# Replacing the planner's greedy order by an explicit table in a long-convolution and linear-attention kernel

## The chip, the cores and the metric

The kernel runs on one core of a Trainium2 chip. The metric is the device time of one execution in microseconds; smaller is better. The core has five engines that run their own instruction streams and wait for each other through semaphores: PE (TensorE, matrix products; its weight loads are listed as PEld), DVE (VectorE), ACT (ScalarE), POOL (GpSimd), and SP (SyncE), which here does nothing but issue DMAs, one after the other in the order in which they are written. Every engine takes its instructions in order: one that waits holds up all that stand behind it on that engine.

## The reference, cut to what matters

Two independent halves are computed and put side by side in the output, 2048 rows of 2 x 576 columns.

```python
def _A_ref(u, log_A_real, A_imag, C_real, C_imag, log_dt, D_skip):   # u: 1 x 2048 x 576
    dt = jnp.exp(log_dt)
    A = -jnp.exp(log_A_real) + 1j * A_imag                            # 576 x 128
    C = (C_real + 1j * C_imag) * dt[:, None]
    P = jnp.exp((A * dt[:, None])[:, :, None] * pos[None, None, :])
    K = 2.0 * jnp.einsum("dn,dnl->dl", C, P).real                     # 576 filters, 2048 long
    y = irfft(rfft(u_t, 2 * L) * rfft(K, 2 * L))[:, :, :L]            # causal convolution
    return y + u * D_skip

def _B_ref(x, wqkv, w_phi, wo):                                       # 32 heads of 18
    q, k, v = split(x @ wqkv)
    pq, pk = q @ w_phi, k @ w_phi
    phi_q = concat(softmax(pq), softmax(-pq)); phi_k = concat(softmax(pk), softmax(-pk))
    kv, z = phi_k^T v, sum(phi_k)
    return ((phi_q kv) / (phi_q z + 1e-6)) @ wo
```

## The kernel before

Half A builds the 576 filters (36 groups of 16 channels: POOL builds phases by doubling, ACT takes sines and exponentials, DVE multiplies, PE sums), transforms filters and input with two-stage Fourier transforms written as small matrix products, multiplies the spectra (16 "products") and transforms back. Half B projects 16 tiles of 128 rows to keys and values, forms one 36 x 19 state per head, and then takes 16 query tiles through projection, feature map, state product, division and output projection. The large projections split each operand into two 32-bit parts of shorter mantissa ("wh" and "wl" are the two parts of the weights) and run as 14 matmuls per tile.

`body` does not emit instructions as it goes. It records 2972 operations in a `Plan`: each has an engine, or a first and a second engine where either may do it, a cost estimate, the buffers it reads and writes, and a function that emits it. `at(name, k)` names the unit of work to which an operation belongs and `step(name)` a step in it. The units that this document speaks of are:

- `fold` (L479 to L503): the key weights multiplied by the feature map's weights, with the first matmuls of the kernel; it waits for the DMAs `e<-in_wkT_dram` and `fT<-in_wphi_dram`.
- `key` and `query` (L602, L663): one tile of half B. `softmax` (L561 to L590) is used by both; its `tt` calls (L446 is where they are recorded) may run on POOL or DVE: `e<-small,e` is the second half of the feature map, `e<-e,small` the scaling of it.
- `group` (L907): one group of 16 filters, after `phases` (POOL, L876 to L892) and `waves` (ACT, L894).
- `product` (L983 to L1055): one sixteenth of a half of the spectra. In its step p2, DVE multiplies (`ac<-us,ps`, L450); in p3 two more operations for each of two `ac` buffers (`ac<-ac`, L446) may run on POOL or DVE; in p4 PE transforms the result back (`ps<-ac,ff`).
- `last` (L1061): the last transform of half A and its store.

`Plan.run` then sets the order. It keeps for each engine the operations whose inputs are there, and at each step starts the one that can start first, by cost estimates, latencies (`LAG`), a due time for each unit (the table `WANT`) shifted for each step (`LEAD`), and five further tuned numbers. Where an operation may run on two engines the planner compares the estimated ends. A buffer's slot is given by the due order, within a window.

One more thing sets the instruction stream: filler matmuls. Where the planner's own clock says that PE would wait for more than 150 ns, `emit` puts matmuls by a tile of zeros (L215, `ps<-ident,zero`, up to 256 columns wide) in front of the operation, into the buffer that this operation overwrites: as many as fit in the wait, counting 114 ns each (228 ns while its clock holds PE for not yet warm), whatever the width of the buffer. They are written into the program as it is built, so on the chip they are run whether PE would have waited there or not.

Of the kernel before, what the change touches and what calls it, by code (L numbers as in the profile page):

```python
# [13 lines left out]
ALU = mybir.AluOpType  # L14
# [144 lines left out]
class Plan:  # L159
# [9 lines left out]
    def __init__(self):  # L169
        self.ops, self.pools, self.free, self.window, self.strict = [], {}, {}, {}, {}  # L170
        self.now, self.unit, self.part = 0.0, None, None

    def tag(self, name, pool, n, window=None):
        self.pools[name], self.free[name] = pool, [0.0] * n
        self.window[name], self.strict[name] = window or n, not window

    def at(self, name, k=0):
        self.now, self.unit, self.part = WANT[name][k], (name, k), None

# [6 lines left out]
    def op(self, eng, cost, fn, r=(), w=(), with_=(), early=0.0, table=None, busy=1.0, lock=False, mode=(128, 128), add=None):  # L186
# [3 lines left out]
        for b in w:  # L190
            deps.update(b.readers)
        k = len(self.ops)
# [11 lines left out]
        self.ops.append([eng, cost, fn, deps, bufs, self.now - early - LEAD.get(self.part, 0.0), table, busy, lock and eng, (self.unit, early, self.part), mode, fill[0] if fill else None, alt, add])  # L204

    def emit(self, k, o, eng, fill=0):
        if fill:
# [6 lines left out]
            for _ in range(fill):  # L214
                self.matmul(t[0:cols, 0:n], self.zero.t[0:rows, 0:cols], self.data.t[0:rows].bitcast(BF16)[:, 0:n], start=not o[13], stop=not o[13], skip_group_check=bool(o[13]))  # L215
        o[2](eng) if o[12] else o[2]()

    def run(self):
        ops = self.ops
        n = len(ops)  # L220
        users = [[] for _ in ops]
        todo = [len(o[3]) for o in ops]
        for k, o in enumerate(ops):
            for d in o[3]:
                users[d].append(k)
        place, seen = {}, {t: 0 for t in self.free}
        low, ahead = {t: 0 for t in self.free}, {t: set() for t in self.free}
        for k in sorted(range(n), key=lambda k: ops[k][5]):
            for b in ops[k][4]:
                if id(b) not in place:  # L230
                    place[id(b)] = seen[b.tag]
                    seen[b.tag] += 1

        def slot(b, more=0):

            fr, p, tag = self.free[b.tag], place[id(b)], b.tag
            if len(fr) <= more:
                return None
            while low[tag] in ahead[tag]:
                ahead[tag].remove(low[tag])  # L240
                low[tag] += 1
            before = p - low[tag] - more
            if before >= self.window[tag]:
                return None
            if before and self.strict[tag] and before - sum(v < p for v in ahead[tag]) >= len(fr):
                return None
            return sorted(fr)[more]

# [14 lines left out]
        self.start = [0.0] * n  # L263
        ready = {e: {} for e in self.LAG}
        table, dma, done, end, mode = None, 0.0, 0, [0.0] * n, None
        self.engine = [o[0] for o in ops]

        def free(k, t):
            ready[ops[k][0]][k] = t
            if ops[k][12]:  # L270
                ready[ops[k][12][0]][k] = t

        def first(e, t, lock):
            s = max(t, at[e])
            return max(s, port["pool" if e == "dve" else "dve"]) if lock and e in port else s
        for k in range(n):
            if not todo[k]:
                free(k, 0.0)
# [828 lines left out]
```

## Time and profile before

| what | value |
|---|---|
| time, median of three runs | 590.35 us |
| the three runs | 590.35, 584.51, 590.45 us |
| the profiled execution | span 585.5 us |
| bytes moved by DMA | 119.26 MB, mean 204 GB/s |

A group's line in the profile gives the line of the kernel, the engine, the operation with its tiles, the number of instructions, their busy time together, the mean time of one, and the idle time of the engine just before them with what ended it. Matmuls overlap, so a mean of 319 ns does not say that a matmul adds 319 ns; the distance between starts does. A busy PE is no proof of useful work here, since the fillers count as busy.

### The profile page before, as it was taken

What the parts mean: (1) busy time and instruction counts of PE and PEld (TensorE: products, weight loads), DVE (VectorE), ACT (ScalarE), POOL (GpSimd) and SP (SyncE); (2) the same over time, 40 slices, a digit from 0 to 9 for tenths busy, and PEclk for the clock granted to TensorE, in tenths of its full rate; (3) what the DMA queues carried; (4) which work ended last, traced back from release to release, by engine and by line L of the source; (5) the groups of instructions that cost most, each with busy time, mean ns of one, the idle gap of its engine ahead of it and who ended that gap; (6) DMA issues with size and microseconds to landing.
All of it is one profiled execution on the core that took longest, in us unless ns stands there. A gap on an engine that the chain in (4) does not pass through costs nothing.

```text
span 585.5 us, 18811 instructions
## 1 busy us (share of the span) xinstructions
PE 558.6 (95%) x7694; PEld 461.4 (79%) x7694; DVE 516.7 (88%) x1110; ACT 392.5 (67%) x672; POOL 239.3 (41%) x385
## 2 busy tenths in 40 slices
PE   5999999999999999898999999999999999999996
PEld 4898899999987679787786776767678786767885
DVE  4799999999999899999899999999978788787751
ACT  5479868687778989488678586998685334432332
POOL 0437366844763446671551448544601210201000
PEclk9899999999999999899999999999999999999999
DMA  8979822550239485226655846885589789997586
GB/s 270 270 254 305 314 89 80 176 160 8 68 94 286 162 289 186 77 88 167 213 207 168 250 148 200 234 247 179 178 242 302 211 234 302 277 303 262 182 260 207
DMA packets 91317, 119.26 MB, mean 204 GB/s; under 512 B 9826, under 2 KB 73186, under 8 KB 91230
## 3 DMA queue, kind: packets, MB, share of 16 engines
q1 hardware_dynamic: 91230, 118.04, 64.9%
q8 instruction: 61, 1.00, 0.7%
q14 instruction: 26, 0.21, 0.1%
HBM read 68.76 MB, written 49.26 MB: 202 GB/s over the span
## 4 chain that ended last, share of the span: by engine, by line
PE 59%; DVE 19%; DMA 9%; ACT 8%; issue 2%; POOL 1%; SPq 1%; ACTq 0%; DVEq 0%
PE ps L431 55%; DVE cs L924 2%; DVE E L925 2%; DMA zi<-dram 2%; PE ps L215 2%; PE ps L678 2%; DVE e L446 1%; DVE ac L450 1%; ACT cs L904 1%; DMA kb<-dram 1%; DMA e<-in_wkT_dram 1%; DVE E L927 1%; ACT cs L903 1%; DVE E L929 1%; DMA dt<-in_ldt_dram 1%
## 5 line engine op out<-in xcount | busy, mean ns | idle before, releaser
L431 PE MATMUL ps<-wh,x 128*128 128x288 f32 (+2 forms) x1008 | 240.7, 319 | 2.3 <-ACT zi L436 1.8
L431 PEld LDWEIGHTS ps<-wh,x 128*128 128x128 f32 x1008 | 173.2, 188 | 12.2 <-issue 3.7
L431 PE MATMUL ps<-wl,x 128*128 128x288 f32 (+2 forms) x560 | 174.9, 313 | 0.0
L888 POOL TENSOR_TENSOR cs<-cs,pi 128x128 int32<-128x128 int32 (+4 forms) x180 | 117.7, 657 | 10.7
L431 PEld LDWEIGHTS ps<-wl,x 128*128 128x128 f32 x560 | 105.7, 189 | 0.7
L579 POOL TENSOR_TENSOR o<-e 128x576 f32<-128x576 f32 x32 | 42.0, 1320 | 98.5 <-ACT e L576 92.2
L918 ACT ACTIVATE ps<-ps 128x512 f32<-128x512 f32 x108 | 57.0, 585 | 11.3 <-PE ps L431 11.1
L924 DVE TENSOR_TENSOR cs<-ps,cs 128x1024 f32<-128x1024 f32 x36 | 43.6, 1212 | 5.5 <-ACT ps L918 5.4
L431 PEld LDWEIGHTS ps<-kvb,fT 126*128 126x128 f32 (+1 forms) x320 | 40.2, 196 | 7.2 <-PE ps L431 1.7
L450 DVE TENSOR_TENSOR ac<-us,ps 128x576 f32<-128x576 f32 x64 | 44.5, 744 | 0.5 <-ACT fT L436 0.5
L898 ACT ACTIVATE cs<-cs 128x1040 f32<-128x1040 int32 x35 | 37.6, 1073 | 10.7 <-POOL cs L888 10.5
L431 PE MATMUL ps<-kvb,fT 126*128 126x133 f32 (+1 forms) x320 | 42.8, 285 | 0.9 <-DVE small L571 0.6
L925 DVE TENSOR_TENSOR E<-ps,cs 128x1024 f32<-128x1024 f32 x36 | 43.5, 1208 | 0.1
L446 POOL TENSOR_TENSOR ac<-ac 128x288 f32<-128x288 f32 x21 | 17.2, 826 | 63.8 <-DVE ac L450 63.8
L431 PEld LDWEIGHTS ps<-E,cs 128*32 128x32 f32 x2304 | 34.5, 110 | 10.4 <-issue 3.9
L431 PE MATMUL ps<-E,cs 128*32 128x64 f32 x2304 | 40.7, 221 | 1.1 <-ACT zi L436 0.7
L576 ACT ACTIVATE e<-e 128x1152 f32<-128x1152 f32 x32 | 37.0, 1173 | 6.6 <-DVE e L446 4.8
L904 ACT ACTIVATE cs<-cs,hp 128x1040 f32<-128x1040 f32 x36 | 41.4, 1149 | 0.0
L215 PE MATMUL ps<-ident,zero 128*128 128x256 bf16 (+6 forms) x230 | 33.1, 292 | 6.5 <-DVE cs L924 4.3
L903 ACT ACTIVATE cs<-cs 128x1040 f32<-128x1040 int32 x36 | 38.3, 1064 | 0.2
L436 ACT ACTIVATE zi<-ps 128x288 f32<-128x288 f32 x73 | 25.1, 417 | 16.1 <-PE ps L431 15.6
L568 DVE TENSOR_REDUCE small<-ps 128x16 f32<-128x288 f32 (+2 forms) x64 | 28.5, 445 | 8.0 <-PE ps L431 7.1
(140 smaller groups left out, 1046.9 us busy)
## 6 DMA issues: line engine op xcount, KB each, us to landing
xd<-x SPq DMA_DIRECT2D x16, 576.0 KB
dram<-zi SPq DMA_DIRECT2D x16, 576.0 KB
x<-xd SPq DMA_DIRECT2D x16, 576.0 KB
dram<-zi SPq DMA_DIRECT2D x32, 288.0 KB
kb<-dram SPq DMA_DIRECT2D x32, 288.0 KB
ub<-dram SPq DMA_DIRECT2D x32, 288.0 KB
dram<-zo SPq DMA_DIRECT2D x32, 288.0 KB
zi<-dram SPq DMA_DIRECT2D x16, 576.0 KB
```

Of the source, the lines that this page charges most:

```text
L215: self.matmul(t[0:cols, 0:n], self.zero.t[0:rows, 0:cols], self.data.t[0:rows].bitcast(BF16)[:, 0:n], start=not o[13], stop=not o[13], ski ...
L431: pe.matmul(o, l, r, start=start, stop=stop, skip_group_check=skip)
L450: op(eng, c_dve(n) if eng == "dve" else c_pool(n), lambda: e.tensor_tensor(dst(), a(), b(), op=alu), r=r, w=w, lock=eng == "pool" or not a ...
L576: op("act", c_act(1152) + 40, lambda: act.activation(e.t, e.t, AF.Exp), r=[e], w=[e], table="exp")
L579: op("pool", c_pool(470), lambda: pool.tensor_tensor(pair.t, e.t[:, :, :, 0:9], e.t[:, :, :, 9:18], op=ALU.add), r=[e], w=[pair], lock=True)
L888: op("pool", c_pool(2 * n * W), lambda n=n, j=j: pool.tensor_tensor(x()[:, :, :, n:2 * n], x()[:, :, :, 0:n], pi.t[:, j:j + 2, gs].bitcast ...
L898: op(("act", "dve"), (c_act(65 * W), c_dve(65 * W)), lambda e, cs=cs, x=x: act.activation(cs.t[:, 0], x(), AF.Abs) if e == "act" else dve. ...
L903: act.activation(cs.t[:, 1], cs.t[:, 1].bitcast(I32), AF.Sin, scale=TURN)
L904: act.activation(cs.t[:, 0], cs.t[:, 0], AF.Sin, scale=-TURN, bias=hp.t)
L918: op("act", c_act(512), lambda: act.activation(ps.t, ps.t, AF.Exp), r=[ps], w=[ps], table="exp")
L924: op("dve", c_dve(64 * W), lambda: dve.tensor_tensor(F(), both(M.t), F(), op=ALU.mult), r=[M, cs], w=[cs])
L925: op("dve", c_dve(64 * W), lambda: dve.tensor_tensor(E.t[:, :, :, 32:64], both(up.t), cs.t[:, :, :, 0:32], op=ALU.mult), r=[up, cs], w=[E])
```

## The change

The operations, their functions and their buffers stay as they are. What `run` decided step by step is now read from a table, `ORDER`: 2972 numbers, each the place of an operation in the order of recording; a star behind a number says that it runs on its second engine. The due times, the step shifts, the windows and the five tuned numbers go. The cost estimates, latencies and the clock that counts them stay, and serve two ends only: they choose the free buffer slot, and they set the number of fillers ahead of a PE operation, by the same rule as before. The clock now also makes each PE operation wait for the two tiles that fillers read, and the first key tile for the clearing of its sum.

```diff
-    def run(self):
+    def run(self, order):
         ops = self.ops
...
-        while done < n:
-            best = None
-            for e, rs in ready.items():
...
-            e, k, s = best
+        for x in order:
+            k, second = int(x.rstrip("*")), x.endswith("*")
             o = ops[k]
+            e, cost = o[5] if second else o[:2]
+            s = max([at[e], *(end[d] for d in o[3])])
             for b in o[4]:
                 if b.t is None:
                     fr = self.free[b.tag]
                     b.t0 = min(fr)
                     fr.remove(b.t0)
-                    ahead[b.tag].add(place[id(b)])
+                    s = max(s, b.t0)
                     b.t = self.pools[b.tag].tile(b.shape, b.dt, name=b.tag, tag=b.tag)
...
-            nf = 0
+            fill = 0
             if e == "pe":
                 t = at[e]
                 if o[11] is not None:
-                    t = max(t, 0.0 if o[13] else o[11].t0, self.zero_at)
+                    t = max(t, 0.0 if o[12] else o[11].t0, self.zero_at)
                     idle(t - at[e])
                     c = FILL if self.warm else 2 * FILL
-                    nf = max(0, min(100, int((s - 150.0 - t) // c)))
+                    fill = max(0, min(100, int((s - 150.0 - t) // c)))
...
-STAY, TURNOVER, NEAR, LEAN_POOL, LEAN_ACT = 37.6104, 135.5510, 109.2559, -92.0902, 57.9818
-LEAD = dict(g1=1412.5796, g2=445.7536, ...
-WANT = dict(
...
+ORDER = """
+384 2 3 0 362 1 363 1313 1312 1316 1317 40 1314 1315 46 1322 5 364* 4 7 12 1225 1321 365* 1281 19 1324 1319 33 41
...
+""".split()
...
     with tc.manual_schedule():
-        pl.run()
+        pl.run(ORDER)
```

What the built programs hold, counted over the whole of each: fillers 230 before, 91 now (up to the first two large projections 79 before and 37 now; in the rest of the kernel 151 and 54). DVE has 1110 operations of its own before and 1064 now, POOL 381 and 429, ACT 584 and 582. Moved from DVE to POOL, net: 19 of `ac<-ac`, 14 of `e<-small,e`, 7 of `e<-e,small` 128x1152, 6 of `e<-e,small` 128x576, 2 of `x<-zo,x`. ACT's table loads are 34 before and 38 now. SP issues the same 395 DMAs.

Three places follow. Names are the program's: `v` and `sel` hold a selection matrix that half A needs first at its first group, `ub<-in_u` an input block of half A, `zo<-in_xT` a tile of half B's input, `zi`, `cs<-in_wv` the value weights, `dt`, `th`, `cre`, `cim` filter parameters. All lines below L460 or so stand two lines earlier in the changed file.

The first place is the head of SP's queue, up to the first two blocks of key weights. Before:

```order
L802 DMA v_85<-in_sel_dram 128x512
L746 DMA ub<-in_u_dram 128x576
L473 DMA zo<-in_xT_dram 128x5x128
L821 DMA dt<-in_ldt_dram 128x96
L823 DMA th<-in_aim_dram 128x96
L823 DMA cre<-in_cre_dram 128x96
L823 DMA cim<-in_cim_dram 128x96
L802 DMA v_115<-in_sel_dram 128x512
L473 DMA zi<-in_wv_dram 128x5x192
L473 DMA cs<-in_wv_dram 128x5x192
L482 DMA fT<-in_wphi_dram 128x630
L486 DMA e<-in_wkT_dram 126x640 x2
```

And the same stretch of SP's queue now:

```order
L471 DMA zo<-in_xT_dram 128x5x128
L821 DMA th<-in_aim_dram 128x96
L819 DMA dt<-in_ldt_dram 128x96
L471 DMA zi<-in_wv_dram 128x5x192
L821 DMA cre<-in_cre_dram 128x96
L821 DMA cim<-in_cim_dram 128x96
L471 DMA cs<-in_wv_dram 128x5x192
L484 DMA e<-in_wkT_dram 126x640
L480 DMA fT<-in_wphi_dram 128x630
L484 DMA e<-in_wkT_dram 126x640
L744 DMA ub<-in_u_dram 128x576
```

Both loads of `sel` and the load of `u` now stand behind the first key weights, which move from the twelfth place to the eighth.

The second place is PE's first work, between the first `fold` blocks and the first large projection. Before, the piece behind the last of nine fillers, up to the first of the next six:

```order
L215 LDWEIGHTS zero
L215 MATMUL ps<-ident,zero 128x256
L431 MATMUL ps<-fT,E 128x126 x5
L431 MATMUL ps<-fT,kvb 128x72 x5
L215 LDWEIGHTS zero
L215 MATMUL ps<-ident,zero 128x256
```

Now, from the first `fold` blocks on:

```order
L429 MATMUL ps<-fT,e 128x126 x10
L215 LDWEIGHTS zero
L215 MATMUL ps<-ident,zero 128x126
L429 MATMUL ps<-fT,E 128x126
L215 LDWEIGHTS zero
L215 MATMUL ps<-ident,zero 128x256
L429 MATMUL ps<-fT,kvb 128x72 x4
L429 MATMUL ps<-fT,E 128x126 x4
L429 MATMUL ps<-ub,w_173 128x288 x4
L429 MATMUL ps<-fT,kvb 128x72
```

One filler stands where nine stood, another one in the middle of the blocks, and an input transform of half A (`ub,w`) has moved between them.

The third place is step p3 in the first products. On DVE before, in the first of them (`ac<-us,ps` is p2, `ac<-ac` is p3; `x` and `fT`, `ot` belong to query tiles that run beside it):

```order
L450 TENSOR_TENSOR ac<-us_4892,ps 128x576 x2
L450 TENSOR_TENSOR x_4941<-ps,x_4941 128x512
L446 TENSOR_TENSOR ac<-ac 128x288
L450 TENSOR_TENSOR x_4941<-ps,x_4941 64x128
L446 TENSOR_TENSOR ac<-ac 128x288
L436 COPY fT<-ps 126x512
L450 TENSOR_TENSOR ac<-us_4893,ps 128x576 x2
L436 COPY fT<-ps 72x256
L446 TENSOR_TENSOR ac<-ac 128x288
L436 COPY ot<-ps 128x288
L446 TENSOR_TENSOR ac<-ac 128x288
```

On POOL now, in the first two products (`cs<-cs,pi` is the doubling of phases of later groups, `o<-e` a sum in a feature map):

```order
L886 TENSOR_TENSOR cs<-cs,pi 128x16x2x16
L444 TENSOR_TENSOR ac<-ac 128x288 x3
L444 TENSOR_TENSOR e<-small,e 128x576
L577 TENSOR_TENSOR o<-e 128x576
L444 TENSOR_TENSOR ac<-ac 128x288 x3
L882 COPY cs<-pi 128x16x2
L444 TENSOR_TENSOR ac<-ac 128x288
L881 MEMSET cs 128x16
L886 TENSOR_TENSOR cs<-cs,pi 128x16x2
```

Four p3 operations stood on DVE among the copies of a query tile; now seven of the eight of two products stand on POOL, nearly in a row. In the first eight products 18 of 32 p3 operations ran on DVE before and 5 do now; in the last eight 25 and 19.

More of the change, by code (lines that the diff above doesn't have):

```diff
@@ L214, in emit @@
             for _ in range(fill):
-                self.matmul(t[0:cols, 0:n], self.zero.t[0:rows, 0:cols], self.data.t[0:rows].bitcast(BF16)[:, 0:n], start=not o[13], stop=not o[13], skip_group_check=bool(o[13]))
-        o[2](eng) if o[12] else o[2]()
-    def run(self):
+                self.matmul(t[0:cols, 0:n], self.zero.t[0:rows, 0:cols], self.data.t[0:rows].bitcast(BF16)[:, 0:n], start=not o[12], stop=not o[12], skip_group_check=bool(o[12]))
+        o[2](eng) if o[5] else o[2]()
+    def run(self, order):
         ops = self.ops
[L220 to L247, printed above, removed]
+        if sorted(int(x.rstrip("*")) for x in order) != list(range(len(ops))):
+            raise RuntimeError("the order does not hold every operation once")
         at = {e: 0.0 for e in self.LAG}
@@ L262, in busy @@
                 self.warm = True
[L263 to L275, printed above, removed]
```

222 lines of the change are left out of this document (129 added, 93 removed).

## The prediction

> **What bounds the kernel now.** I read the page first for who is busy, then the chain of waits, then stretches of the span engine by engine, the fillers by themselves, and the rows of the operations that change engines.
>
> From the page of the kernel before: the span, each engine's busy time, PE and DVE in 40 slices, the clock that PE was granted, the start of the chain that ended last, and the fillers' group.
>
> ```profile
> span 585.5 us, 18811 instructions
> PE 558.6 (95%) x7694; PEld 461.4 (79%) x7694; DVE 516.7 (88%) x1110; ACT 392.5 (67%) x672; POOL 239.3 (41%) x385
> ...
> PE   5999999999999999898999999999999999999996
> ...
> DVE  4799999999999899999899999999978788787751
> ...
> PE 59%; DVE 19%; DMA 9%; ACT 8%; issue 2%; POOL 1%; SPq 1%; ACTq 0%; DVEq 0%
> ...
> L215 PE MATMUL ps<-ident,zero 128*128 128x256 bf16 (+6 forms) x230 | 33.1, 292 | 6.5 <-DVE cs L924 4.3
> ```
>
> PE is the bound, though not through all of its 558.6 us: 33.1 us of them are fillers, which compute nothing. With the 26.9 us in which PE is idle (585.5 - 558.6), PE does no useful work in 60.0 us. The change leaves every real matmul, so those 60 us are what an order can win or add to. The stretches say where they lie: all instructions first, then the fillers (L215) alone, five stretches each.
>
> ```profile
> core 0: us, PE busy (x) PEld busy (x) DVE busy (x) ACT busy (x) POOL busy (x), PEclk, DMA share, GB/s
> 0.00:14.00 14.00, 7.34 (x43) 5.63 (x44) 6.43 (x18) 7.07 (x10) 0.78 (x10) 0.97 0.86 265
> 14.00:50.00 36.00, 36.00 (x224) 33.72 (x224) 30.92 (x81) 24.18 (x41) 15.48 (x25) 0.92 0.85 274
> 50.00:150.00 100.00, 99.90 (x1619) 91.62 (x1618) 96.99 (x202) 77.75 (x117) 61.34 (x97) 1.00 0.45 147
> 150.00:440.00 290.00, 275.49 (x4247) 221.04 (x4246) 276.16 (x569) 228.61 (x385) 143.04 (x237) 0.99 0.61 186
> 440.00:585.50 145.50, 139.88 (x1567) 109.35 (x1566) 106.25 (x243) 54.84 (x123) 18.62 (x17) 0.99 0.83 254
> ```
>
> ```profile
> core 0: us, PE busy (x) PEld busy (x), PEclk, DMA share, GB/s
> 0.00:14.00 14.00, 7.00 (x42) 5.27 (x42) 0.97 0.86 265
> 14.00:50.00 36.00, 5.62 (x37) 3.96 (x37) 0.92 0.85 274
> 50.00:150.00 100.00, 0.00 (x0) 0.00 (x0) 1.00 0.45 147
> 150.00:440.00 290.00, 20.50 (x151) 14.11 (x151) 0.99 0.61 186
> 440.00:585.50 145.50, 0.00 (x0) 0.00 (x0) 0.99 0.83 254
> ```
>
> Three regimes. Up to 50 us PE waits for the first data: in the first 14 us all but one of its 43 matmuls are fillers, and 5.62 us go in fillers after that. From 50 to 150 us PE is full (99.90 of 100). From 150 to 440 us PE loses 14.5 us idle and 20.5 us in fillers, 35.0 in all, and the engine with least slack is DVE: 276.16 of 290 us busy. From there to the end PE loses 5.6 us and there is no filler.
>
> **The change, part by part.**
>
> *The start.* The chain that ended last, in order of time, begins with DMAs (start, length, what):
>
> ```profile
> 0.74 2.77 DMA v<-in_sel_dram
> ...
> 6.23 7.30 DMA e<-in_wkT_dram
> 13.67 4.61 PE ps L431 x20
> 18.27 1.84 PE ps L215 x9
> 20.11 2.19 PE ps L431 x20
> ...
> 25.39 2.29 PE ps L215 x20
> ```
>
> The first key weights are the twelfth issue, at 6.23 us; the first issue is at 0.74, so one takes (6.23 - 0.74) / 11 = 0.50 us. As eighth issue they go out 4 x 0.50 = 2.0 us sooner. By bytes it is more (KB of each issue, from the list of DMA issues):
>
> ```profile
> ub<-in_u_dram SPq DMA_DIRECT2D x16, 288.0 KB
> ...
> v<-in_sel_dram SPq DMA_DIRECT2D x3, 256.0 KB
> ```
>
> Two loads of `sel` (`v`) and one of `u`, 256 + 256 + 288 KB, no longer run ahead, and at the 265 GB/s of that stretch they take 3.1 us. Between 2.0 and 3.1 I take 2.5 us for the first real matmul. The 42 fillers ahead of it are hidden by that wait, so the ten that go there are worth nothing.
>
> *Fillers from 14 to 50 us.* 37 become 5. A filler costs 5.62 / 37 = 0.152 us here, so at most 32 x 0.152 = 4.9 us go; nothing, if PE now waits bare for the same blocks of weights. Since the blocks come 2.5 us sooner, half of the wait should go: 2.4 us.
>
> *Fillers from 150 to 440 us.* 151 become 54, so 97 go. By the stretch's row one costs 20.50 / 151 = 0.136 us; by the longest run in the chain above 2.29 / 20 = 0.115 us. That is 11.1 to 13.2 us, and I take 12. None of it is won if the wait behind the fillers stays, and this is the term to defend. The fillers' own row names DVE as what ended most of the idle time that was left before them (4.3 of 6.5 us), and DVE has 13.8 us of slack in these 290. These are the rows of what leaves DVE, then of the same operations on POOL (instructions, busy time, mean ns of one, idle time before):
>
> ```profile
> L446 DVE TENSOR_TENSOR e<-e,small 128x1152 f32<-128x1152 f32 x16 | 23.6, 1477 | 0.0
> ...
> L446 DVE TENSOR_TENSOR e<-small,e 128x576 f32<-128x576 f32 x26 | 20.2, 776 | 0.2
> L446 DVE TENSOR_TENSOR ac<-ac 128x288 f32<-128x288 f32 x43 | 20.2, 490 | 0.1
> ...
> L446 DVE TENSOR_TENSOR e<-e,small 128x576 f32<-128x576 f32 x12 | 9.9, 827 | 0.2
> ```
>
> ```profile
> L888 POOL TENSOR_TENSOR cs<-cs,pi 128x512 int32<-128x512 int32 x36 | 41.7, 1159 | 2.4
> ...
> L446 POOL TENSOR_TENSOR ac<-ac 128x288 f32<-128x288 f32 x21 | 17.2, 826 | 63.8 <-DVE ac L450 63.8
> ...
> L446 POOL TENSOR_TENSOR e<-small,e 128x576 f32<-128x576 f32 x6 | 7.2, 1207 | 3.3 <-DVE small L571 3.3
> ...
> L446 POOL TENSOR_TENSOR e<-e,small 128x576 f32<-128x576 f32 x4 | 5.1, 1270 | 17.5 <-DVE small L450 13.5 <-DVE zo L436 3.9
> ```
>
> DVE gets rid of 19 x 0.490 + 14 x 0.776 + 7 x 1.477 + 6 x 0.827 = 35.5 us over the kernel, some 7% of its 516.7. The 13 `ac<-ac` of the first eight products, which lie in this stretch, are 6.4 us of it. So DVE's need there can fall by the 12 us by which the stretch is to shrink; the cover that a full DVE gave to PE's waits goes with it. What is late next is POOL: it takes on 19 x 0.826 + 14 x 1.207 + 6 x 1.270 = 40.2 us and seven operations of a form that it never ran, between 7 x 1.27 (the half as wide one) and twice that: 9 to 18 us. Its 239.3 us become about 293. It was idle for half of this stretch (143.04 of 290), so I cost it at nothing; the price without that cover is the second rival.
>
> *PE's bare idle time*, 14.5 us in this stretch and 5.6 at the end, I leave as it is: the table removes foreseen waits, and these were not foreseen, or fillers would stand there. Bounds: all 14.5 may go, or as much come in.
>
> *ACT.* Four more table loads. Their two largest groups:
>
> ```profile
> L903 ACT ACT_TABLE_LOAD x14 | 18.0, 1283 | 0.2
> L918 ACT ACT_TABLE_LOAD x13 | 16.7, 1283 | 1.2 <-PE ps L431 0.9
> ```
>
> 4 x 1.283 = 5.1 us on an engine that has 290 - 228.61 = 61 us free in the middle: nothing, and 5.1 us lost if each stands before a sine for which DVE waits.
>
> *SP and the last stretch.* The issues are the same 395, in another order. SP takes them in order, so a store that waits for its copy holds the loads behind it; in the last stretch the DMA engines are busy for 0.83 of the time, and there I expect neither gain nor loss, -3 to +6 us by PE's own 5.6 us of slack.
>
> The sum: 2.5 + 2.4 + 12 = 16.9 us less than 585.5, a span of 568.6 us. The runs shown are 584.51 to 590.45 with a median of 590.35; the profiled execution lies 1.0 above the lowest and 4.9 below the median. The median to come may sit on either side of such a step, so I add 1.4 us and forecast **570.0 us**.
>
> **The rivals.**
>
> *Bare waits in place of fillers.* The table is built with the same estimates as the planner; where those are wrong, PE still waits, only idle. For it: a full DVE in the middle, and PE's idle 26.9 us, which the estimates missed already. Against it: DVE does lose work. Only the start is then won: 585.5 - 2.5 = 583 us, with the 1.4 us 584.4, no measurable change. If half of the 2.4 + 12 us returns, 577.
>
> *PE cools down.* Fillers keep PE busy; without them a long bare wait may cost more than itself. The longest wait of PE, and the longest run of fillers in the middle (from the list of PE's waits: total, times, longest; and from the chain):
>
> ```profile
> PE ps L431 <- DMA e<-in_wkT_dram: 5.1, 1, 5.1
> ```
>
> ```profile
> 360.32 2.92 PE ps L215 x26
> ```
>
> After that wait of 5.1 us the next 20 matmuls took 4.61 us, 20 of their kind shortly after (half of them narrower) 2.19: 2.4 us lost on top. If six waits came back bare and long, 6 x 2.4 = 14.4 us would eat the gain: 584 us. Against it: the longest run in the middle covers 2.92 us, less than the 5.1 that did cost. The Trainium skill, "TensorE: Matmul & The Clock Gate", section "What's actually happening", says that PE falls to half its clock after an idle window of about 3.4 us and comes back after as long a busy one; the trace agrees at its one long wait (twice the time behind it), and by this rule, too, a bare wait of 2.92 us is just short of costing anything.
>
> *POOL becomes the bound; slower.* In the third place of the change seven p3 operations stand on POOL among phases and sums of feature maps. With all four on POOL, a product's p4 comes 4 x 0.826 - 2 x 0.826 = 1.7 us later than with two on each engine; with a chain of phases ahead (five links, each as wide again as the one before; the last alone takes 1.159 us, so some 2.3 us in all, an estimate) 4.0 us. Over the first eight products that is 32 us: 585.5 - 16.9 + 32 = 601 us, if nothing hides it. It decides once PE waits more than 16.9 / 8 = 2.1 us a product for POOL. Against it: PE has query tiles and groups to do in between, and POOL was idle for half of the stretch. The rows of before show another price: of the two `ac<-ac` on POOL in one product, the one that ran beside the same operation on DVE took longer (start, length):
>
> ```profile
> 328.47 0.81 POOL L446 TENSOR_TENSOR ac<-ac 128x288 f32<-128x288 f32 x1 [1.30 <-DVE ac L450]
> ...
> 330.38 1.02 POOL L446 TENSOR_TENSOR ac<-ac 128x288 f32<-128x288 f32 x1
> ```
>
> 0.21 us for each of the 48 operations that POOL gains would be 10 us of POOL's time, hidden like the rest. The Trainium skill, "SBUF — State Buffer", section "Who interferes with whom", says that a DVE instruction with two inputs in SBUF and a POOL instruction that reads SBUF lock each other out for a whole instruction; the trace shows 0.21 us here, less than the 0.490 of DVE's `ac<-ac`. By the rule the moves also take such instructions off DVE, so it speaks for neither side.
>
> *More than the fillers.* If DVE's need alone sets the middle, it shrinks by more, up to all 35.0 us that PE loses there; with half of the bare waits gone as well (7 us) and all 4.9 us of the early fillers it is 585.5 - 2.5 - 4.9 - 13.2 - 7 = 558 us, with the whole 35.0 us 543.
>
> **How the numbers follow.** The forecast, 562 to 578 us: 0.55. More won, under 562: 0.14. Half or less, 578 to 584: 0.12. Bare waits, no change: 0.10; PE cooling, no change: 0.02. POOL, slower: 0.07. About 1% is what a measurement of this kernel can tell from no change, so faster is below 584.4: 0.55 + 0.14 + 0.12 = 0.81; the same up to 596.3: 0.10 + 0.02 = 0.12; slower 0.07. Two in ten may be left out: half of the cases below 562 and the upper part of the last two, which gives 554 to 586 us.
>
> **What would show it.** Right: the fillers' group at 91 and some 12 us; the first real matmul near 11 us; DVE near 485 us and POOL near 295 us busy; PE idle no more than about 27 us in the whole span; the last group of filters done some 17 us sooner. Wrong: idle time of PE released by DVE or POOL where fillers stood (bare waits); p4's matmuls waiting for POOL's `ac` (the second rival); a granted clock under 0.9 outside the first 50 us.

## The result, and the profile after

The changed kernel takes 583.37 us (median of 20 runs, 577.81 to 590.03); before took 589.67 us beside it (20 runs). The ratio is 0.9898, 95% interval 0.9873 to 0.9924: about 1% shorter, 6.3 us where 16.9 were forecast. All ratios here leave out the slower executions of both kernels, so they differ a little from those of the medians. The profiled execution has a span of 578.1 us against 585.5. That of after belongs to an execution of 580.1 us, 3.3 under the median.

The page of the kernel after, span, busy time, and PE and DVE in 40 slices:

```profile
span 578.1 us, 18504 instructions
...
PE 539.4 (93%) x7555; PEld 445.8 (77%) x7555; DVE 499.5 (86%) x1064; ACT 392.4 (68%) x674; POOL 288.6 (50%) x433
...
PE   3999899999889998989999999999999989889996
...
DVE  4899899999889899999999999999978779778662
```

DVE's busy time falls by 17 us and POOL's rises by 49. PE's slices now show gaps (8 instead of 9) in the 5th, 11th, 12th and 16th slice, where before had none, and in the 33rd, 35th and 36th. The same five stretches as before, all instructions:

```profile
core 0: us, PE busy (x) PEld busy (x) DVE busy (x) ACT busy (x) POOL busy (x), PEclk, DMA share, GB/s
0.00:14.00 14.00, 5.29 (x40) 5.12 (x41) 6.78 (x23) 6.50 (x10) 0.71 (x9) 1.00 0.81 228
14.00:50.00 36.00, 35.25 (x273) 33.24 (x274) 33.54 (x77) 28.27 (x45) 21.05 (x35) 1.00 0.88 288
50.00:150.00 100.00, 93.76 (x1582) 85.55 (x1579) 95.32 (x195) 80.31 (x120) 65.89 (x95) 1.00 0.45 147
150.00:440.00 290.00, 277.28 (x4245) 222.46 (x4244) 266.22 (x550) 233.74 (x399) 171.70 (x267) 1.00 0.64 196
440.00:578.10 138.10, 127.83 (x1425) 99.44 (x1423) 97.64 (x225) 43.61 (x102) 29.29 (x28) 0.99 0.80 247
```

And the fillers (L215) alone in them:

```profile
0.00:14.00 14.00, 3.52 (x32) 3.35 (x32) 1.00 0.81 228
14.00:50.00 36.00, 1.02 (x5) 0.58 (x5) 1.00 0.88 288
...
150.00:440.00 290.00, 8.05 (x54) 5.17 (x54) 1.00 0.64 196
```

Read against the same rows of before, PE's time without real work (idle and fillers) goes from 13.7 to 12.2 us in the first stretch (14.00 - 5.29 + 3.52), from 5.6 to 1.8 in the second and from 35.0 to 20.8 in the fourth. But it rises from 0.1 to 6.2 us between 50 and 150 us, and from 5.6 to 10.3 in the last stretch. The stretches end at fixed times, not at the same work, so here beside them is when PE starts its last step of the n-th unit of a kind to be done (us, worked out from the starts of PE's instructions in the two traces; a group pair is two groups of 16 filters):

| PE's last step of | before | after | after - before | change since the row above |
|---|---|---|---|---|
| the 1st key tile | 55.0 | 48.9 | -6.1 | -6.1 |
| the 16th key tile | 206.3 | 203.5 | -2.8 | +3.3 |
| the 18th group pair | 454.7 | 443.3 | -11.4 | -8.6 |
| the 16th `last` | 579.2 | 571.6 | -7.6 | +3.8 |

So 14.7 us are won at the start and in the middle, and 7.1 are given back: 3.3 while the keys are done, 3.8 in the last stretch. Up to 1.7 of the 8.6 us are no matter of order: in this execution of before PE ran at half clock from 241.8 to 245.2 us, and after's did not. PE's waits of after from 50 to 150 us (line, released by: total, times, longest):

```profile
PE ps L429 <- issue: 2.1, 2, 1.9
PE ps L429 <- DVE E L923: 1.6, 2, 1.2
PE ps L429 <- DVE zi L434: 0.8, 1, 0.8
PE ps L429 <- DVE e L448: 0.7, 1, 0.7
PE ps L429 <- DVE E L927: 0.6, 2, 0.5
```

These rows are 5.8 of the 6.2 us. Wherever an engine is named, it is DVE, for 3.7 us ("issue" names none). From 440 us on it is three single waits, at 513, 468 and 499 us:

```profile
PE ps L429 <- DVE zo L434: 1.6, 1, 1.6
PE ps L429 <- DMA kb<-dram: 1.5, 1, 1.5
PE ps L429 <- ACT x L437: 1.2, 1, 1.2
```

One more difference is on DVE itself. Small operations of the filter parameters (128x96, all in SBUF), in before:

```profile
L834 DVE TENSOR_SCALAR pi<-th 128x96 f32<-128x96 f32 x18 | 3.5, 227 | 0.0
...
L834 DVE TENSOR_SCALAR dt<-mx 128x96 f32<-128x96 f32 x6 | 1.7, 286 | 0.0
...
L450 DVE TENSOR_TENSOR mn<-mn,dt 128x96 f32<-128x96 f32 x6 | 1.6, 272 | 0.1
```

and in after:

```profile
L832 DVE TENSOR_SCALAR pi<-th 128x96 f32<-128x96 f32 x18 | 7.4, 413 | 0.0
...
L448 DVE TENSOR_TENSOR mn<-mn,dt 128x96 f32<-128x96 f32 x6 | 3.6, 608 | 0.0
...
L832 DVE TENSOR_SCALAR dt<-mx 128x96 f32<-128x96 f32 x6 | 3.4, 567 | 0.0
```

The same instructions take about twice as long on average beside a busier POOL. The mean mixes two kinds: of the 18 `pi<-th` of after, the 11 that no POOL instruction overlaps in time take 193 ns on average, and the 7 that one overlaps 760 ns (198 to 2291).

### The profile page after: what moved, and what is told of

Read it like the earlier page. It is cut to its first block, busy times and chain, and to the rows that moved or that the text cites. A ratio compares the mean times of both kernels' runs of the same rounds, so it can differ in the third digit from the quotient of the medians.

```text
span 578.1 us, 18504 instructions
## 1 busy us (share of the span) xinstructions
PE 539.4 (93%) x7555; PEld 445.8 (77%) x7555; DVE 499.5 (86%) x1064; ACT 392.4 (68%) x674; POOL 288.6 (50%) x433
## 5 line engine op out<-in xcount | busy, mean ns | idle before, releaser
L886 POOL TENSOR_TENSOR cs<-cs,pi 128x128 int32<-128x128 int32 (+4 forms) x180 | 116.4, 650 | 10.1
L916 ACT ACTIVATE ps<-ps 128x512 f32<-128x512 f32 x108 | 60.0, 588 | 12.9 <-PE ps L429 12.6
L444 POOL TENSOR_TENSOR ac<-ac 128x288 f32<-128x288 f32 x40 | 32.8, 831 | 55.9 <-DVE ac L448 45.5
L429 PEld LDWEIGHTS ps<-kvb,fT 126*128 126x128 f32 (+1 forms) x320 | 38.8, 189 | 5.3 <-issue 3.1
L429 PE MATMUL ps<-kvb,fT 126*128 126x133 f32 (+1 forms) x320 | 41.4, 278 | 0.2
L429 PE MATMUL ps<-sel,mg 128*128 128x512 f32 x108 | 38.0, 430 | 3.6 <-DVE wl L496 1.6
L444 POOL TENSOR_TENSOR e<-small,e 128x576 f32<-128x576 f32 x20 | 23.3, 1167 | 33.7 <-DVE e L448 27.3
L429 PE MATMUL ps<-kb,fk 128*64 128x288 f32 x256 | 35.7, 414 | 4.2 <-DVE zo L434 1.6
L444 POOL TENSOR_TENSOR e<-e,small 128x576 f32<-128x576 f32 (+1 forms) x17 | 27.0, 1590 | 23.5 <-DVE small L448 17.1
L901 ACT ACTIVATE cs<-cs 128x1040 f32<-128x1040 int32 x36 | 38.3, 1064 | 0.2
```

Source lines behind the costliest of these rows:

```text
L429: pe.matmul(o, l, r, start=start, stop=stop, skip_group_check=skip)
L444: op(eng, [c_dve(n[0]) if e == "dve" else c_pool(n[1]) for e in eng], lambda e: (dve if e == "dve" else pool).tensor_tensor(dst(), a(), b( ...
L886: op("pool", c_pool(2 * n * W), lambda n=n, j=j: pool.tensor_tensor(x()[:, :, :, n:2 * n], x()[:, :, :, 0:n], pi.t[:, j:j + 2, gs].bitcast ...
L901: act.activation(cs.t[:, 1], cs.t[:, 1].bitcast(I32), AF.Sin, scale=TURN)
L916: op("act", c_act(512), lambda: act.activation(ps.t, ps.t, AF.Exp), r=[ps], w=[ps], table="exp")
```

## The experiments

Each time stands beside runs of the kernel before on the same chip. The ratio to compare with is that of after, 0.9898. Where an experiment on before's order has an edit of the changed kernel's text, that order is written as a table for the changed kernel, which gives the instruction streams of before; line numbers then differ by some lines.

**No fillers planned.** In each kernel the number of fillers is set to zero.

```diff
-                    nf = max(0, min(100, int((s - 150.0 - t) // c)))
+                    nf = 0
```

> The kernel before without its 230 fillers; all else in the same order. Theory A (a filler is a price: what is taken out of PE's stream is won, the premise of the prediction): 33 us of fillers go, of which the 7 ahead of the first matmul are hidden, so 590 becomes about 564. Theory B (fillers only stand in waits that last as long without them): within 1% of before, PE's idle time rises by about the 33 us that the fillers took, or the kernel is some us slower where PE cools.

Measured: 661.89 us, ratio 1.1225 (1.1172 to 1.1279). This is no measure of the fillers. Where a planner decides as it goes, the clock that counts fillers also tells it whether PE is warm, so without them it put the work in another order and on other engines (DVE has 1116 operations instead of 1110). The granted clock is 0.94 in the profiled execution. The run leaves its question open.

The same line in after, where the table holds the order whatever the clock says:

```diff
-                    fill = max(0, min(100, int((s - 150.0 - t) // c)))
+                    fill = 0
```

> The changed kernel without its 91 fillers. Theory A: 12.6 us of fillers go, 3.5 of them hidden at the start: 583 becomes about 574. Theory B: 583 within 3 us, PE's idle time rises from 38.7 to about 50 us.

Measured: 580.49 us, ratio 0.9844 (0.9798 to 0.9891). Slots of buffers may differ too, so the next pair is cleaner.

**Engines and order apart.** The order of after with the engine that before gave to each operation that may run on DVE or POOL (62 go back to DVE, 14 to POOL), and the reverse. Only stars in the table change; operation 53 is one of them:

```diff
-... 52* 1230* 53 206 55 37 ...
+... 52* 1230* 53* 206 55 37 ...
```

> The changed kernel's table with every operation that may run on DVE or POOL on the engine that it had before (62 go back to DVE, 14 to POOL); the order stays. Theory C (what POOL takes on slows DVE's operations with two inputs in SBUF, so the moves are worth little): 583 within 3 us or faster, and DVE's small parameter operations are back at a mean near 270 ns from 350. Theory D (the moves are what wins; DVE sets the middle): slower, 590 to 600.

> The kernel before in its own order, with every operation that may run on DVE or POOL on the engine that the changed kernel gives it. Theory C: no faster than before, 586 to 595. Theory D: faster, 573 to 583, since DVE sheds the same work.

Measured: 599.03 us, ratio 1.0148 (1.0096 to 1.0201), and 596.97 us, ratio 1.0133 (1.0086 to 1.0179). The two pages, after's order first:

```profile
span 593.5 us, 18729 instructions
...
PE 555.8 (94%) x7676; PEld 458.0 (77%) x7676; DVE 527.8 (89%) x1112; ACT 394.4 (66%) x674; POOL 241.7 (41%) x385
```

```profile
span 594.5 us, 18989 instructions
...
PE 569.0 (96%) x7790; PEld 468.4 (79%) x7790; DVE 494.6 (83%) x1062; ACT 392.7 (66%) x672; POOL 288.0 (48%) x433
```

Neither part wins anything alone; by the ratios both lose more than 1%. The new order needs the shorter DVE: with DVE back at 527.8 us it is 2.5% slower than after. And a shorter DVE (494.6 us) gives the old order nothing: from PE's last step of the 1st key tile to that of the 16th it needs 161.2 us, before 151.3. What it waits for there was not found; PE's waits name POOL only once, for 0.3 us. Two things go with the order in these runs and are not taken apart: 182 further operations that after gives to the other of ACT and DVE, and the fillers, which the clock counts anew (212 in the first run, 326 in the second).

**Fillers counted but not sent.** The clock counts the fillers as before, so order, engines and slots are unchanged, and only the matmuls by zeros are missing. Before and after:

```diff
-            self.emit(o, e, nf)
+            self.emit(o, e, 0)
```

```diff
-            self.emit(o, e, fill)
+            self.emit(o, e, 0)
```

> The kernel before with its fillers counted by the planner's clock as ever, so that order, engines and buffer slots stay the same, and not emitted: only 230 matmuls of zeros are missing. Theory A (a filler is a price): about 564. Theory B (fillers stand in waits that last as long without them, and PE does not cool): 585 to 592, PE's idle time up by about 30 us. Theory B2 (they hold PE's clock): slower, over 595, with a granted clock under 0.97.

> The changed kernel with its 91 fillers counted and not emitted, order and slots the same. Theory A: about 574. Theory B: 580 to 585. Theory B2: over 588.

Measured: 588.45 us, ratio 0.9977 (0.9948 to 1.0006), and 580.0 us, ratio 0.985 (0.9801 to 0.990). All 230 fillers of before, 33.1 us of PE's busy time, are worth 0.2% (by the interval no more than 0.5%), and the 91 of after some 0.5%, less than their intervals tell apart. Much of the wait that they fill is there without them: PE's idle time in before rises from 26.9 to 45.1 us. The profile of before without fillers shows a second thing, from 190 to 250 us (columns as above; the granted clock is the third number from the right):

```profile
190.00:250.00 60.00, 52.59 (x642) 43.46 (x643) 51.68 (x111) 46.86 (x80) 32.14 (x50) 0.86 0.53 170
```

Before, with its fillers, and after have in the same 60 us:

```profile
190.00:250.00 60.00, 55.01 (x840) 46.80 (x837) 55.95 (x116) 48.44 (x83) 32.64 (x53) 0.97 0.54 176
```

```profile
190.00:250.00 60.00, 55.26 (x957) 46.99 (x956) 56.26 (x121) 51.51 (x95) 43.26 (x64) 1.00 0.55 175
```

Without fillers PE loses (1 - 0.86) x 60 = 8.4 us of clock here, with them 1.8, in after none. So in this execution a filler is not idle ballast, since part of what it costs in busy time it saves in clock. How much it saves on average is not shown: the granted clock over the whole of this execution, 0.983, is near the lowest of its twelve (0.982 to 0.993). What is shown is the sum, which is close to zero.

**The small operations of the parameters.** 126 operations of DVE on the filter parameters become a maximum over one element of one input, to see whether POOL holds that up, too. What they computed is left out by it, so the filters are others.

```diff
-            tt("dve", z or (lambda: dst.t), lambda: x.t, lambda: y.t, alu, [x, y], [dst], BW)
+            op("dve", c_dve(BW), lambda: dve.tensor_reduce((z() if z else dst.t), x.t[:, :, None], axis=AX.X, op=ALU.max), r=[x, y], w=[dst], lock=True)
...
-            op("dve", c_dve(BW, True), lambda: dve.tensor_scalar(z() if z else dst.t, x.t, s0, s1, op0=o0, **k), r=[x], w=[dst], lock=True)
+            op("dve", c_dve(BW, True), lambda: dve.tensor_reduce(z() if z else dst.t, x.t[:, :, None], axis=AX.X, op=ALU.max), r=[x], w=[dst], lock=True)
```

> The kernel before with DVE's 126 small operations on the filter parameters (96 columns, one or two inputs in SBUF) replaced by a maximum over one element of their first input, which has one input in SBUF and takes about as long by itself; the filters are wrong by it. Order and POOL stay. Theory P (DVE and POOL lock each other out, and the change has more of it): the small operations fall from a mean near 270 to near 200 ns, and the time by 2 to 6 us, to 584 to 588. Theory T (the order is tight, the lockout only fills waits): no change, within 2 us of before.

> The changed kernel with the same replacement. Theory P: it wins more here than in the kernel before, 7 to 13 us, to 570 to 576, and PE's idle time from 50 to 150 us falls from 6.2 to under 3. Theory T: 580 to 584, the distance to the kernel before with the same replacement stays 4 to 8 us.

Measured: 587.51 us, ratio 0.9955 (0.9925 to 0.9986), and 580.33 us, ratio 0.9846 (0.981 to 0.9883). In the order of after the replaced instructions now take (413 and 567 ns before):

```profile
L832 DVE TENSOR_REDUCE pi<-th 128x96 f32<-128x96 f32 x18 | 4.2, 240 | 0.0
...
L832 DVE TENSOR_REDUCE dt<-mx 128x96 f32<-128x96 f32 x6 | 1.5, 242 | 0.0
```

That takes 10.7 us from DVE (499.5 to 488.8) and 4.3 in before's order (516.7 to 512.4), but both kernels gain about the same half per cent. So being held up by POOL is real, as these rows show, and it is not what separates the two orders.

**Less for DVE in the key tiles.** If DVE is what the new order waits for in the first 200 us, it should gain from a shorter DVE there, and before should not. First the smallest value is left out:

```diff
-            op("dve", c_dve(DH * m), lambda: dve.tensor_reduce(ends.t[:, :, 1], v(), axis=AX.X, op=ALU.min), r=[p], w=[ends])
+            op("dve", c_dve(DH * m), lambda: dve.tensor_reduce(ends.t[:, :, 1], v(), axis=AX.X, op=ALU.min) if total else
+               dve.memset(ends.t[:, :, 1], 0.0), r=[p], w=[ends])
```

> The order and the engines of before. In the key tiles each smallest value over the features (the second of the two reductions on DVE, 540 ns for 21 heads and 350 ns for 11, so 0.89 us a tile and 14.3 us in 16 tiles) is replaced by a memset to zero in the same place: the second exponential then subtracts nothing, and the division by its sum makes up for it. Theory D (in after DVE is what the stretch from 14 to 150 us waits for, and PE is not; in before PE is full there): before gains little from it, 0 to 3 us, since PE had 0.1 us of 100 free in 50 to 150 us; ratio to before 0.995 to 1.000. Theory S (a shorter DVE helps whatever the order, because DVE's queue also sets the middle): 5 to 10 us gained, ratio 0.983 to 0.991.

> The same replacement in the order and with the engines of after. Theory D: the 6.2 us in which PE has no work between 50 and 150 us fall to 2 or less, a unit's last step there comes 4 to 8 us sooner, and the end comes 4 to 8 us sooner than after's own: ratio to before 0.976 to 0.984 (after alone 0.990), so the gap to the same edit in before grows to 1.3% or more. Theory S: the same gain as in before, 5 to 10 us, so that the gap between the two orders stays at about 1.0%. If PE's idle time in 50 to 150 us stays at 4 us or more, DVE's length isn't what it waits for, and theory D falls.

Measured: 588.43 us, ratio 0.9973 (0.9934 to 1.0012), and 579.6 us, ratio 0.9809 (0.977 to 0.9849). The stretch from 50 to 150 us, before's order and after's:

```profile
50.00:150.00 100.00, 100.00 (x1620) 91.88 (x1619) 92.22 (x203) 77.93 (x118) 61.90 (x97) 1.00 0.44 142
```

```profile
50.00:150.00 100.00, 95.81 (x1591) 88.69 (x1590) 88.06 (x200) 81.50 (x122) 67.01 (x97) 0.98 0.46 149
```

The times come out as theory D has them; the idle time of PE does not. It falls from 6.2 to 4.2 us and not to 2 or less, and with 4 us or more the theory was to fall: by this mark it does. Even that fall is no pure gain, since PE runs at half clock from 54.3 to 57.7 us here (0.98 in the row) and so is busy for up to 1.7 us longer with the same work. So twice the dose, the sum of the features and its reciprocal as well; the key features are then not divided by their sums:

```diff
-        op("dve", c_dve(576), lambda: dve.tensor_reduce(sm.t.rearrange("p h s -> p s h"), pair.t, axis=AX.X, op=ALU.add), r=[pair], w=[sm])
+        op("dve", c_dve(576), lambda: dve.tensor_reduce(sm.t.rearrange("p h s -> p s h"), pair.t, axis=AX.X, op=ALU.add) if total else
+           dve.memset(sm.t, 1.0), r=[pair], w=[sm])
...
-            op("dve", 470, lambda: dve.reciprocal(sm.t, sm.t), r=[sm], w=[sm])
+            op("dve", 470, lambda: dve.memset(sm.t, 0.1), r=[sm], w=[sm])
```

> The order and engines of before. In the key tiles alone three DVE instructions become small memsets: the smallest value (0.89 us a tile), the sum over the features (0.74 us) and the reciprocal of that sum (0.54 us), about 1.85 us a tile net and 30 us in 16 tiles, all in the first 205 us. The key features are therefore not divided by their sums; everything else is computed. Theory D (DVE's load is what after's order waits for in the first 150 us, and before's order, with PE full there, cannot use a shorter DVE): 0 to 4 us gained; ratio 0.993 to 1.000. Theory S (the load is worth the same in either order): 8 to 14 us gained, ratio 0.976 to 0.986.

> The same three memsets in the order and with the engines of after. Theory D: PE's time without work in 50 to 150 us falls below 3 us (6.2 in after, 4.2 with the smallest value alone left out), the 16th key tile's last step comes 5 us or more sooner than in after, and the end 8 to 12 us sooner than after's own: ratio 0.970 to 0.977, and the gap to the same edit in before grows to 1.8% or more. Theory S: the gap stays at 1.0%. Third way, W: what DVE holds up was already given free by the smallest value alone, so it ends as that kernel did, ratio 0.978 to 0.984, with 4 us idle left in 50 to 150 us; then what is left there is not DVE's load but the order itself.

Measured: 591.19 us, ratio 1.0004 (0.997 to 1.0037), and 580.98 us, ratio 0.9829 (0.9776 to 0.9883). Before's order and after's:

```profile
50.00:150.00 100.00, 100.00 (x1620) 91.89 (x1619) 83.67 (x202) 77.68 (x117) 62.26 (x100) 1.00 0.45 145
```

```profile
50.00:150.00 100.00, 95.50 (x1591) 88.59 (x1590) 85.66 (x199) 81.23 (x122) 66.57 (x98) 0.98 0.46 150
```

In before, DVE's load falls by 13 us in this stretch (96.99 to 83.67) and the time does not move: PE, busy all the time, is the bound. In after the second dose adds nothing to the first that can be told (theory W), and some 4 us of idle PE are left; half clock, from 146.0 to 149.4 us, has its part in this row as well. The tiles themselves are the cleaner measure. From PE's last step of the 1st key tile to that of the 16th it is 154.6 us in after, 152.4 with one dose and 151.9 with two; in before's order 151.3, 151.2 and 151.7. The run that changes after only behind 440 us (the next one) has 154.7, so this measure repeats. Of the 3.3 us that after's order loses here, DVE's load thus accounts for 2.2 to 2.7, and the rest is open.

**Three waits of the last stretch.** The PE steps that wait in the rows above (the two p2 of product 12, the p1 of product 10, the two p2 of product 15) come later on PE, behind work that does not hang on them. Of the table, at the first of them:

```diff
-... 764 2770 977 978 779 2772 2777 2739 979 780 2913 2771 ...
+... 764 977 978 779 979 780 2913 2770 2772 2739 2777 2771 ...
```

> After with three PE steps of the last stretch one place later, behind work that does not hang on them: the two multiplications of product 12 with kb (the first waits 1.5 us for a DMA at 468 us), the first step of product 10 (waits 1.2 us for a buffer that ScalarE empties, at 499 us), and the two multiplications of product 15 (wait 1.6 us for a buffer that VectorE empties, at 513 us). The engines stay. Theory L (the 4.3 us of these three waits are single late releases next to ready work): PE's idle time from 440 us on falls from 10.3 to about 6 us, and the end comes 3 to 4 us sooner; ratio to before 0.983 to 0.986. Theory Q (every other step stands as tightly, so the waits only move to the steps that now come later): no gain, -1 to +3 us against after; ratio 0.988 to 0.995.

Measured: 583.1 us, ratio 0.9867 (0.9825 to 0.9908): no gain that can be told from after. The last stretch and its longest waits:

```profile
440.00:582.20 142.20, 133.77 (x1464) 103.39 (x1463) 100.49 (x230) 45.30 (x106) 29.32 (x28) 0.99 0.80 246
```

```profile
PE ps L440 <- ACT fT L445: 1.1, 1, 1.1
PE ps L440 <- DMA zi<-dram: 0.7, 1, 0.7
...
PE ps L440 <- DMA kb<-dram: 0.3, 1, 0.3
```

The wait for `kb` shrinks to 0.3 us, and others come up, for steps that wait for ACT and for `zi`. With the 18 fillers that the clock adds (2.7 us), PE is without work for 11.1 us here, 10.3 before this edit. The ratio, 0.9867, lies between what theory L (0.983 to 0.986) and theory Q (0.988 to 0.995) have, and its interval takes in both; what speaks for Q is that PE's time without work did not fall.

**What helps, put together.** The smallest value left out and the fillers not sent, in the order of after.

```diff
-            self.emit(o, e, fill)
+            self.emit(o, e, 0)
...
-            op("dve", c_dve(DH * m), lambda: dve.tensor_reduce(ends.t[:, :, 1], v(), axis=AX.X, op=ALU.min), r=[p], w=[ends])
+            op("dve", c_dve(DH * m), lambda: dve.tensor_reduce(ends.t[:, :, 1], v(), axis=AX.X, op=ALU.min) if total else
+               dve.memset(ends.t[:, :, 1], 0.0), r=[p], w=[ends])
```

> The order of after with the smallest value left out of the key tiles' softmax (as in the run before last batch's) and the 91 fillers not sent to PE. The output is the same, since a sum divides the shift out. If the two edits add up, 0.9809 less the 0.5% that the unsent fillers gave: ratio 0.974 to 0.978, some 576 us. If a filler costs nothing and its 0.5% was spread between runs: 0.979 to 0.983.

Measured: 577.47 us, ratio 0.9771 (0.9723 to 0.982), the shortest of all: 2.3% under before, 1.3% under after. That the two add up (0.974 to 0.978) is not shown, for the interval also takes in the other case, in which the fillers add nothing. The sum divides the shift out of the second softmax, so what is computed is the same as long as its exponentials stay in range.

## Why the prediction was right in direction and wrong in size

Two steps of the sum failed: the price of the 97 fillers in the middle (12 us, where 8.6 were won there), and the stretch from 50 to 150 us, which stands in it at nothing and lost 3.3. A third loss, 3.8 us in the last stretch, stood in it at nothing as well, and its cause stays open. The start won 1.2 us more than its two terms. Beside this, the sum was taken from a span, 585.5 us, and the times are some 2 us longer than their spans (580.1 against 578.1); from before's median of 589.67 the same 16.9 us lead to 572.8 and not to 570.0.

- *The start* (2.5 + 2.4 us). Right in sum, and a little small: PE is 6.1 us ahead after the first key tile. Its parts were not as forecast. The first real matmul comes at 12.23 us instead of 13.67, so 1.4 of the 2.5 us came from there and the rest from the fillers and waits between 14 and 50 us (5.6 to 1.8 us without work). The prediction moved up the first key weights alone; PE now waits for another load, which before stood ahead of them and now stands behind:

```profile
PE ps L429 <- DMA fT<-in_wphi_dram: 7.2, 1, 7.2
```

- *The middle* (12 us). The mechanism was right, the size was not: from the 16th key tile to the last group PE gains 8.6 us. The step that failed is the price, "That is 11.1 to 13.2 us", 97 fillers at what one takes on PE. A filler's length is not what its absence wins. Not sending all 230 in before changed the time by 0.2%: PE's idle time rises by 18.2 us, and in the profiled execution its clock falls. That the 8.6 us come from waits which the order and the moves to POOL shortened, for which fillers are a mark and not a measure, is what is left, and no run shows it directly; the separate runs show that the whole gain needs both parts.
- *From 50 to 150 us* I wrote "PE is full" and costed nothing. The row that I quoted for it also has DVE at 96.99 of 100 us. Two engines were near their limit: work that PE could start 6 us sooner met a DVE with 3 us to spare. This is where 3.3 us came back, and with a shorter DVE after's order does the key tiles 2.2 to 2.7 us faster, before's does not. The times of the whole point the same way: after's order gains (ratio 0.9809 and 0.9829, 0.9898 without), before's does not clearly (0.9973 and 1.0004). Between the two orders the gap grows from 1.0% to 1.64% (0.9809 / 0.9973) and 1.75% (0.9829 / 1.0004), that is from 6 us to about 10. That would be some 4 us of the 10 that were missing, a loose estimate, since each ratio has an interval of about 0.4% to either side and the growth, 0.6 to 0.7%, is hardly more than its noise. PE's idle time, the mark set for it, did not bear the theory out.
- *POOL at no cost.* It has not become the bound (288.6 us busy; PE's list of waits does not name it, that of its weight loads does three times, for 0.3 us at most), as forecast. But it was not free. The rows of the four kinds of operation that leave DVE fall from 73.9 to 43.2 us, 30.7 where 35.5 were forecast, for those that stay take longer each (`e<-small,e` 964 ns instead of 776). The 126 small operations and the reciprocals on the parameters take 47.2 us instead of 37.7. So DVE's busy time is 499.5 us, and not the 485 of the sign. Sparing 126 of them gave half a per cent in either order. The prediction's "0.21 us for each" had charged this to POOL alone.
- *Bare idle time, left as it is,* and *the last stretch, neither gain nor loss.* PE's idle time rose from 26.9 to 38.7 us, and 3.8 us were lost in the last stretch. That is just outside the -3 to +6 given, if these count gains as the other terms do. Moving its three longest waits won nothing that can be told. Why this stretch takes longer than before's was not found.
- *The rivals.* "Bare waits in place of fillers" is the nearest, with its variant "if half returns, 577": the waits did not come back where fillers had stood but at places that had none before. "PE cools down" is not what ate the gain: by its records after runs at full clock from 16.7 to 576.5 us. At the start it does cool, although its rows there say 1.00, for the trace has no record of the clock before 16.7 us: behind the wait of 7.2 us the `ps<-fT,e` matmuls start 213 ns apart up to 16.4 us, and 111 ns apart from 25.9 us on. Before does the same behind its wait of 5.1 us (213 ns apart up to 17.9 us). Cooling elsewhere is seen where only the fillers are taken from before, and not as the prediction had it. In before without fillers, from 196 us on, in steps of 2 us:

```profile
196.00:198.00 2.00, 0.83 (x4) 0.29 (x2) 2.00 (x3) 2.00 (x4) 0.00 (x0) 1.00 0.56 160
198.00:200.00 2.00, 1.64 (x18) 0.81 (x22) 2.00 (x5) 2.00 (x6) 1.27 (x1) 0.57 0.00 1
200.00:202.00 2.00, 2.00 (x62) 1.83 (x56) 2.00 (x6) 0.55 (x2) 0.35 (x3) 0.50 0.72 205
202.00:204.00 2.00, 2.00 (x9) 0.96 (x8) 1.30 (x3) 0.61 (x3) 1.76 (x4) 0.50 0.60 241
204.00:206.00 2.00, 2.00 (x11) 1.75 (x11) 0.62 (x1) 2.00 (x6) 1.84 (x3) 0.73 0.54 134
206.00:208.00 2.00, 1.77 (x73) 1.39 (x73) 1.67 (x3) 1.11 (x3) 0.43 (x1) 1.00 0.96 345
```

From 193.4 us on PE is idle for 2.0 of 4.8 us, in three pieces of 0.5 to 0.9 us, and then runs at half its clock for 6.8 us, which loses 3.4. The Trainium skill, "TensorE: Matmul & The Clock Gate", section "What's actually happening", ties the fall to an idle window of about 3.4 us; here the trace shows it after shorter pieces with work between them, and the measurement decides. The prediction used that rule to call waits of under 3 us free. One wait can be enough, too: in after with the smallest value left out, PE waited from 51.7 to 53.5 us, 1.7 us, and ran at half clock from 54.3 to 57.7 us (matmuls of one tile 314 ns apart instead of 175); waits of 1.9 us at 146 us in after and of 2.6 us in before without fillers were followed by none.

What stays open: the idle PE from 50 to 150 us that a shorter DVE does not remove, and the last stretch. No run tried another order for them.

## What to carry to other kernels

Before an order is credited with a gain, read every engine's busy share in the stretch where the gain must pass: a second engine at 97% can take back what the first is given, and that is tested cheaply by making the second one shorter under both orders. Measure it by the time from one fixed piece of work to another, since idle time mixes with the clock: a slower PE is less idle. Count filler or warm-up work at nothing until a run without it has been made, with everything else held fixed; where a planner reads the fillers' clock, taking them out changes the order as well. An order and its assignment of engines are one thing: either half of this change alone made the kernel 1.3 to 1.5% slower. And check a granted clock of 1.00 at the start of a profile against the distance between matmuls of one shape.

## What the runs showed of the hardware that had not been expected

- PE fell to half its clock (0.50) after three idle pieces of at most 0.9 us in 4.8 us. In the same run it kept 1.00 through a single wait of 2.6 us at 361 to 363 us. In after with the smallest value left out, a single wait of 1.7 us at 52 us was followed by 3.4 us at half clock.
- POOL holds up DVE operations with one input as well: `pi<-th`, a TENSOR_SCALAR of one tile, went from 227 to 413 ns on average beside a busier POOL (193 ns where no POOL instruction overlaps it, 760 where one does). The same tile read by a TENSOR_REDUCE took 240 ns beside the same POOL.
